# Expert rows and activations transposed by DMA on the SyncE queue, two blocks at a time, in a linear-attention and mixture-of-experts kernel

## The chip, the cores and the metric

The kernel runs on one core of a Trainium2 chip. The metric is the device time of one execution in microseconds (us). TensorE is called PE in the profile (PEld is its weight load), VectorE DVE, ScalarE ACT, GpSimd POOL, SyncE SP.

## The reference

Linear attention (8 batches, 8 heads, 576 positions, head size 64) feeds a mixture of 8 experts. Cut to what matters:

```python
k_p, q_p = phi(k), phi(q)             # relu(x)*cos and relu(x)*sin of the position
kv = einsum('bhsf,bhsd->bhfd', k_p, v); z = k_p.sum(axis=2)
attn = einsum('bhsf,bhfd->bhsd', q_p, kv) / (einsum('bhsf,bhf->bhs', q_p, z) + 1e-6)
x = attn.transpose(0, 2, 1, 3).reshape(4608, 512)
logits = x @ w_gate                   # 8 experts
e = argmax(logits); g = softmax(logits)[e]
# each expert takes at most 1152 tokens, in token order
out[i] = g[i] * (relu(x[i] @ w1[e]) @ w2[e])     # w1 512x1024, w2 1024x512; 0 if not taken
```

## The kernel before

All work is written as operations with a cost, a priority and the tiles that they read and write. A planner (`Plan.schedule`) simulates the engines with these costs, picks the order on each engine, and the program is emitted in that order. Each engine then runs its own list in order. `PHI` is a table of priority offsets by kind of operation. `Slots` is a pool of rotating buffers; a `Ver` is one use of a slot.

The attention works batch by batch. SP loads q, k and v of a batch (line 437, six loads of 576 KB). ACT and DVE scale k and v (lines 452 to 465), PE makes the key-value product (line 535), transposes q (line 493), and applies it (line 603); ACT and DVE bring the result to `num` (lines 613, 617). The routing (lines 658 to 764) finds each token's expert and its place; DVE writes the scaled rows as bf16 to `xg` (line 786), and POOL scatters them into a DRAM buffer `xd`, ordered by expert, 514 elements a row: 512 values and a row number (line 796).

The expert part works on 43 blocks of 128 rows. 20 blocks (table `a`) can be formed when six batches are scattered; the other 23 (table `b`) wait for the last two batches and for `pads`, eight writes of zero rows behind each expert's end (ACT, line 928). For each block:

- SP fetches 128 rows from `xd` into `xr` (line 994); POOL copies the row numbers out (line 998).
- PE transposes the rows, four 128x128 pieces (line 1003), and ACT or DVE copies them from PSUM to a unit buffer `un` (line 1007).
- For each half m of the 1024 hidden columns: PE multiplies with w1 (up, line 1023), ACT or DVE applies relu into `h` (lines 1032, 1034), PE transposes h (turn, line 1041), ACT or DVE copies it to `un` (line 1047).
- PE multiplies with w2 (down, line 1067), ACT or DVE copies the result (line 1072), POOL scatters it to the output (line 1081).

All ups come before the downs. The weights are cast to bf16 while POOL loads them, in halves of eight pieces of 512 KB each: w1a (line 945, during the attention), w1b (after the attention's buffers are given back, `swap`, line 1124), w2's first half (line 956), and w2's second half in w1a's place, once the last first-half up is done.

```python
def f_turn(m):
    def f():
        t_ps = tl(tvs[m], [P, 512], FP32, "ps")[:].bitcast(BF16)
        for x in range(4):
            nc.tensor.transpose(out=t_ps[:, x * P:(x + 1) * P], in_=hvs[m].tile[:, x // 2, x % 2, :],
                                identity=identb[:])
    return f
```

Of the kernel before, what the change touches and what calls it, by code (L numbers as in the profile page):

```python
# [28 lines left out]
    "G": 0.31, "KV": 0.33, "P": 0.35, "Q": -0.14, "T": -0.36, "carry": 1.34, "count": -1.01, "down": 0.6,  # L29
    "end": -3.84, "fetch": 0.26, "gout": 1.98, "ix": 1.87, "kva": 0.07, "load": -0.87, "pad": -0.91,  # L30
    "pre": -0.09, "relu": -1.78, "reluq": -0.77, "rq": 8.8, "scat": -0.24, "seen": -0.1, "tab": 0.69,
    "tmp": 1.28, "tsb": 1.62, "turn": -1.07, "up": -0.52, "vt": 17.49, "w1": 1.81, "w2": 0.68, "warm": -0.07,
    "wg": -0.36, "xT": -5.44, "xturn": -10.62,
# [3 lines left out]
class Slots:  # L37


    def __init__(self, name, n, fifo=True):  # L40
        self.name, self.n, self.fifo = name, n, fifo
        self.holder = [None] * n
        self.vers, self.given = [], 0

# [14 lines left out]
class Plan:  # L59
# [30 lines left out]
    def schedule(self, window=0.25, switch=0.15, sticky=0.6):  # L90
# [11 lines left out]
        while done < len(self.ops):  # L102
            best = {}
            cands = []
            for o in ready:
                t = o.avail
                ok = True
                for v in o.vers:
                    if v.slot is not None:
                        t = max(t, v.ready)  # L110
                    else:
                        ts = []
                        for h in v.slots.holder:
                            if h is None:
                                ts.append(0.0)
                            elif all(u.start is not None for u in h.uses):
                                ts.append(max(u.end for u in h.uses))
# [27 lines left out]
            for v in o.vers:  # L145
                if v.slot is None:
                    opts = []
                    for i, h in enumerate(v.slots.holder):
                        if h is None:
                            opts.append((0.0, i))  # L150
                        elif all(u.start is not None for u in h.uses):
                            opts.append((max(u.end for u in h.uses), i))
# [8 lines left out]
            if o.dma:  # L161
                dma_free = max(dma_free, o.end) + o.dma
                o.end = dma_free + 1.6
# [19 lines left out]
def kernel(  # L183
# [35 lines left out]
    U0, U1, U2 = 4, 41, 42  # L219
# [42 lines left out]
    xrS = Slots("xr", 4)  # L262
    hS, yS, uS = Slots("h", 4, False), Slots("y", 3, False), Slots("un", U0 + U1 + U2, False)
# [5 lines left out]
    v_t = [early.tile([P, HB * VH + HB * J * VX], FP32, name=f"v{i}") for i in range(vS.n)]  # L269
# [11 lines left out]
    nc.vector.memset(zrow[:], 0.0)  # L281

# [69 lines left out]
    for i in range(vS.n):  # L352
        nc.gpsimd.memset(v_raw(i)[:, :, VH - 2:VH], 0.0)
# [17 lines left out]
    identb = const.tile([P, P], BF16, name="identb")  # L371
# [17 lines left out]
    def count_1():  # L389
        nc.vector.tensor_scalar(out=m64_i[:], in0=col_i[:], scalar1=D - 1, scalar2=None, op0=ALU.bitwise_and)  # L390
        nc.vector.tensor_copy(out=m64[:], in_=m64_i[:])
        nc.vector.tensor_copy(out=identb[:], in_=ident[:])
# [27 lines left out]
    def load(b, name, u):  # L420
# [9 lines left out]
        def f():  # L430
            if name == "v":
                m = v_raw(ver.slot)[:, 2 * u:2 * u + 2, 0:J * D]
            elif name == "k":
                m = tl(ver, [P, HB, J, D], FP32, "early")[:, 2 * u:2 * u + 2, :, :].rearrange("p c j d -> p c (j d)")
            else:
                m = tl(ver, [P, 2, J, D], FP32, "early")[:].rearrange("p c j d -> p c (j d)")
# [5 lines left out]
    def attention(b):  # L442
# [37 lines left out]
        def q_relu(u, qr):  # L480
            def f():
                t = tl(qr, [P, J, 2, D], FP32, "early")
                nc.vector.tensor_scalar(out=t[:].rearrange("p j c d -> p c j d"), in0=loaded[b, "q", u].tile[:],  # L483
# [340 lines left out]
    def tab_ops(tag, n, b, prio):  # L824
# [17 lines left out]
        def add(fn, cost=0.1, **kw):  # L842
            keys = [("tab", tag)]
            op(kw.pop("eng", "DVE"), cost, fn, r=[("carry", b)] + kw.pop("r", []), w=keys + kw.pop("w", []), prio=prio,
               **kw).tag = ("tab", tag)
# [78 lines left out]
        def s_pad(e):  # L924
            def f():
                r0 = nc.values_load(T["end"][0:1, e:e + 1], engines=[ACTE], min_val=e * REG, max_val=e * REG + N,
                                    skip_runtime_bounds_check_because=INRANGE)
                zi = nc.scalar.dma_start(out=xd[bass.ds(r0, P), :], in_=zrow[:])
# [6 lines left out]
        for e in range(E):  # L935
            o = op("ACT", 0.95, s_pad(e), r=[("end",)], prio=prio, dma=0.4, after=[state["seen"]])
# [4 lines left out]
    def w1_load(n, e, prio, after):  # L941
        def f():
            if w1h[n] is None:
                w1h[n] = pools["mid"].tile([P, E, G, FH], BF16, name="w1b")
            nc.gpsimd.dma_start(out=w1h[n][:, e, :, :],
                                in_=moe_w1[e].rearrange("(g p) f -> p g f", p=P)[:, :, n * FH:(n + 1) * FH])
        op("POOL", 1.2, f, w=[("w1", n)], prio=prio, dma=2.95, after=after).tag = ("w1", n, e)
# [3 lines left out]
    def w2_load(n, e, prio, after):  # L951
# [6 lines left out]
        op("POOL", 1.2, f, w=[("w2", n)], prio=prio, dma=2.8, after=after).tag = ("w2", n, e)  # L958


    def unit(ver):

        if ver.tile is None:
            s = ver.slot
            where = "moe" if s < U0 else "mid" if s < U0 + U1 else "end"
            ver.tile = pools[where].tile([P, G, P], BF16, name=f"un{s}", tag=f"un{s}")
        return ver.tile

    def block(i):
        tag, n = ("a", i) if i < NA else ("b", i - NA)  # L970
        pr = 20.0 + i
        xv, yv, yp_ = Ver(uS), Ver(yS), Ver(pS)
        hvs, pvs, tvs, hts = ([Ver(s_), Ver(s_)] for s_ in (hS, pS, aS, uS))
# [18 lines left out]
        def f_fetch():  # L992
            xr = tl(xrv, [P, XW], BF16, "moe")
            early_read(nc.sync.dma_start(out=xr[:], in_=xd[bass.ds(row(SP), P), :]))

        def f_ids():
            ids["t"] = const.tile([P, 2], BF16, name=f"ids{i}")
            nc.gpsimd.tensor_copy(out=ids["t"][:], in_=xrv.tile[:, DT:XW])  # L998

        def f_xturn():  # L1000
            x_ps = tl(xpv, [P, 512], FP32, "ps")[:].bitcast(BF16)
            for g in range(G):
                nc.tensor.transpose(out=x_ps[:, g * P:(g + 1) * P], in_=xrv.tile[:, g * P:(g + 1) * P],  # L1003
                                    identity=identb[:])

        def f_xT(eng):
            (nc.scalar.copy if eng == "ACT" else nc.vector.tensor_copy)(  # L1007
                out=unit(xv)[:].rearrange("p g s -> p (g s)"), in_=xpv.tile[:].bitcast(BF16)[:, 0:DT])

        xrv, xpv = Ver(xrS), Ver(aS)  # L1010
        op("SP", 0.75, f_fetch, r=[("table", tag)], w=[("xr", i)], vers=[xrv], prio=pr - 10, dma=0.4,
           after=gate).tag = ("fetch", i)
        op("POOL", 0.15, f_ids, r=[("xr", i)], w=[("ids", i)], vers=[xrv], prio=pr).tag = ("ids", i)
        op("PE", 0.24, f_xturn, r=[("xr", i)], w=[("xps", i)], vers=[xrv, xpv], prio=pr - 3, mode="full",
           ).tag = ("xturn", i)
        op("ACT", 0.5, f_xT, r=[("xps", i)], w=[("xT", i)], vers=[xpv, xv], prio=pr - 3, alt=("DVE", 0.38)).tag = ("xT", i)

        def f_up(m):
            def f():
                e1 = expert()  # L1020
                hp = tl(pvs[m], [P, 2, 512], FP32, "ps")[:, 0, :]
                for g in range(G):
                    nc.tensor.matmul(out=hp, lhsT=xv.tile[:, g, :], rhs=w1h[m][:, bass.ds(e1, 1), g, :],  # L1023
# [3 lines left out]
        def f_relu(m):  # L1027
            def f(eng):
                h = tl(hvs[m], [P, 2, 2, P], BF16, "moe")
                src = pvs[m].tile[:, 0, :].rearrange("p (g q i) -> p g i q", g=2, i=2)  # L1030
                if eng == "ACT":
                    nc.scalar.activation(out=h[:], in_=src, func=ACT.Relu)  # L1032
                else:
                    nc.vector.tensor_scalar(out=h[:], in0=src, scalar1=0.0, scalar2=None, op0=ALU.max)
            return f

        def f_turn(m):
            def f():
                t_ps = tl(tvs[m], [P, 512], FP32, "ps")[:].bitcast(BF16)
                for x in range(4):  # L1040
                    nc.tensor.transpose(out=t_ps[:, x * P:(x + 1) * P], in_=hvs[m].tile[:, x // 2, x % 2, :],  # L1041
                                        identity=identb[:])
            return f

        def f_turned(m):
            def f(eng):
                (nc.scalar.copy if eng == "ACT" else nc.vector.tensor_copy)(  # L1047
                    out=unit(hts[m])[:].rearrange("p f s -> p (f s)"), in_=tvs[m].tile[:].bitcast(BF16)[:, 0:512])
            return f

        for m in range(2):
            pm = pr + 60 * m
            op("PE", 0.89, f_up(m), r=[("xT", i), ("w1", m)], w=[("h", i, m)], vers=[xv, pvs[m]], prio=pm, mode="full",
# [3 lines left out]
            op("PE", 0.24, f_turn(m), r=[("hr", i, m)], w=[("t", i, m)], vers=[hvs[m], tvs[m]], prio=pm - 3,  # L1057
               mode="full").tag = ("turn", i, m)
            op("DVE", 0.38, f_turned(m), r=[("t", i, m)], w=[("hT", i)], vers=[tvs[m], hts[m]], prio=pm,
               alt=("ACT", 0.5)).tag = ("hT", i, m)  # L1060
# [140 lines left out]
```

## Time and profile before

| | us |
|---|---|
| median of 3 runs | 362.04 (358.96 to 363.56) |
| profiled execution | 362.18 |
| its span | 360.4 |
| PE busy | 317.5 (88%) |
| ACT, DVE, POOL busy | 202.5, 187.3, 126.9 |
| mean granted PE clock | 0.965 |

The span runs from the first to the last instruction that the profiler saw; 1.8 us lie around it. A busy PE counts modelled ends of pipelined matmuls. Idle time of an engine that is not the bound costs nothing, so each stage is read by itself: the loads of the first batches, the attention, the ups, the downs.

### The profile page before, as it was taken

How to read it: one execution, taken by the hardware profiler on the slowest of the kernel's cores; microseconds unless marked ns; L12 is line 12 of the kernel's file. 1: busy time of each engine (PE TensorE's matmuls, PEld its weight loads, DVE VectorE, ACT ScalarE, POOL GpSimd, SP SyncE). 2: the span in 40 equal slices, each digit the busy share in tenths (PEclk: the TensorE clock that was granted, in tenths of full speed). 3: DMA queues.
4: the chain of work that ended last, by engine and by line, in shares of the span. 5: the costliest groups of instructions: out<-in, count | busy, mean ns of one | idle time of the engine just before them, and what ended most of it. 6: DMA issues, size and time to landing. Idle time of an engine off the chain costs nothing.

```text
span 360.4 us, 9576 instructions
## 1 busy us (share of the span) xinstructions
PE 317.5 (88%) x3344; PEld 208.9 (58%) x3368; DVE 187.3 (52%) x546; ACT 202.5 (56%) x450; POOL 126.9 (35%) x189
## 2 busy tenths in 40 slices
PE   5779798999989998883998889999999999999991
PEld 1668687878778787642555445555555444444440
DVE  5777889888898888787374435443333000000000
ACT  3588898989698754643444444555554333333330
POOL 5000424252807252657223222320000455555552
PEclk9899899999999899996899999999999999999997
DMA  4999939596995768599999996499100244342230
GB/s 156 394 391 387 344 118 341 181 360 144 382 292 191 119 120 132 148 179 246 207 225 213 215 201 124 76 211 211 27 3 0 94 162 156 146 163 113 92 132 0
DMA packets 38542, 66.62 MB, mean 185 GB/s; under 512 B 3903, under 2 KB 18655, under 8 KB 38498
## 3 DMA queue, kind: packets, MB, share of 16 engines
q0 software_dynamic: 18096, 31.00, 39.6%
q1 hardware_dynamic: 19250, 33.98, 27.4%
q10 hardware_dynamic: 1152, 1.05, 1.1%
q8 instruction: 29, 0.48, 0.5%
q14 instruction: 15, 0.12, 0.1%
HBM read 67.56 MB, written 17.06 MB: 235 GB/s over the span
## 4 chain that ended last, share of the span: by engine, by line
PE 43%; DMA 16%; ACT 10%; DVE 10%; issue 9%; POOL 7%; SPq 2%; ACTq 1%; POOLq 1%; DVEq 0%
PE p L1023 18%; PE p L1067 10%; PE p L603 7%; POOL out_dram L1081 6%; DMA xr<-xd 6%; PE a L1041 5%; DMA v<-in_v_dram 4%; DMA km<-in_k_dram 3%; ACT km L452 3%; DVE num L617 3%; DVE xg L786 2%; ACT v L463 2%; DMA w1a<-in_moe_w_dram 2%; PE a L1003 2%; DMA xd<-zrow 1%
## 5 line engine op out<-in xcount | busy, mean ns | idle before, releaser
L1067 PE MATMUL p<-w,un 128*128 x337 | 74.2, 379 | 0.5 <-issue 0.2
L796 POOL DMA_INDIRECT xd<-xg,si x40 | 45.4, 1135 | 81.9 <-DVE xg L786 64.8
L1032 ACT ACTIVATE h<-p 128x512 bf16<-128x512 f32 x65 | 38.9, 598 | 35.0 <-PE p L1023 32.2
L1067 PEld LDWEIGHTS <-un 128*128 128x128 bf16 x344 | 33.6, 98 | 40.4 <-issue 0.5
L603 PE MATMUL p<-kva,rq 64*128 64x146 f32 x640 | 51.7, 305 | 2.3 <-DVE num L617 0.6
L1072 ACT COPY y<-p 128x512 f32<-128x512 f32 x42 | 24.6, 585 | 48.0 <-PE p L1067 46.9
L1047 DVE COPY un<-a 128x512 bf16<-128x512 bf16 x66 | 27.9, 423 | 43.0 <-PE a L1041 42.9
L603 PEld LDWEIGHTS p<-kva,rq 64*128 64x128 f32 x640 | 44.8, 196 | 8.3 <-DVE num L617 4.6
L1023 PEld LDWEIGHTS <-un 128*128 128x128 bf16 x344 | 32.3, 98 | 28.9 <-issue 6.8
L1023 PE MATMUL p<-w1a,un 128*128 x162 | 43.8, 390 | 2.9 <-issue 1.4
L617 DVE SCALAR_TENSOR_TENSOR num<-p,tant,tmp 128x292 f32<-128x292 f32 (+1 forms) x80 | 39.9, 519 | 11.3 <-ACT tmp L613 10.7
L1023 PE MATMUL p<-w1b,un 128*128 x165 | 43.1, 378 | 1.1 <-issue 0.8
L535 PE MATMUL p<-v,km 64*64 64x132 f32 x1152 | 36.0, 279 | 5.7 <-DMA v<-in_v_dram 4.8
L1081 POOL DMA_INDIRECT out_dram<-y,ids x20 | 19.6, 979 | 58.9 <-ACT un L1047 44.6
L535 PEld LDWEIGHTS p<-v,km 64*64 64x64 f32 x1152 | 33.8, 136 | 7.9 <-issue 7.5
L613 ACT COPY tmp<-p 128x292 f32<-128x292 f32 (+1 forms) x77 | 30.8, 401 | 12.8 <-PE p L603 7.4
L1041 PEld LDWEIGHTS <-h 128*128 128x128 bf16 x344 | 25.2, 99 | 17.7 <-ACT h L1032 3.1
L1041 PE MATMUL a<-identb,h 128*128 128x128 bf16 x344 | 31.8, 221 | 0.7 <-ACT un L1007 0.5
L452 ACT ACTIVATE km<-km,cosn 128x256 f32<-128x256 f32 (+1 forms) x67 | 27.9, 485 | 1.9 <-DMA km<-in_k_dram 1.9
L1081 POOL DMA_INDIRECT out_dram<-y,ix x23 | 22.3, 972 | 16.9 <-ACT y L1072 16.9
L493 PE MATMUL a<-ident,qr 128*128 128x128 f32 x144 | 24.5, 291 | 3.1 <-DVE qr L483 1.2
L998 POOL COPY ids<-xr 128x2 bf16<-128x2 bf16 x43 | 8.8, 214 | 51.7 <-DMA xr<-xd 51.4
(169 smaller groups left out, 345.3 us busy)
## 6 DMA issues: line engine op xcount, KB each, us to landing
v<-in_v_dram SPq DMA_DIRECT2D x16, 576.0 KB, 8.8
km<-in_k_dram SPq DMA_DIRECT2D x16, 576.0 KB, 7.2
qm<-in_q_dram SPq DMA_DIRECT2D x16, 576.0 KB, 9.2
w<-in_moe_w_dram POOLq DMA_DIRECT2D x16, 512.0 KB, 8.1
xr<-xd SPq DMA_DIRECT2D x43, 128.5 KB, 5.2
w1a<-in_moe_w_dram POOLq DMA_DIRECT2D x8, 512.0 KB, 6.0
w1b<-in_moe_w_dram POOLq DMA_DIRECT2D x8, 512.0 KB, 8.8
xd<-zrow ACTq DMA_DIRECT2D x8, 128.5 KB, 7.3
```

The costliest lines, as they stand in the source:

```text
L452: nc.scalar.activation(out=kk, in_=kk, func=ACT.Relu, scale=cosn[:, j:j + 1])
L535: nc.tensor.matmul(out=kv_v[c * D:(c + 1) * D, 2 * o + u, :, :], lhsT=km.tile[rows, 2 * u + c, j, :], rhs=both, start=(j == 0), stop=(j == ...
L603: nc.tensor.matmul(out=p_ps[:, a, o, 0:2 * KW], lhsT=rq[u].tile[a * D:(a + 1) * D, o, col:col + P], rhs=kva.tile[a * D:(a + 1) * D, 2 * o ...
L613: (nc.scalar.copy if eng == "ACT" else nc.vector.tensor_copy)(out=t[0:rows], in_=by_t(0))
L617: nc.vector.scalar_tensor_tensor(out=num.tile[0:rows, c, u * HB:(u + 1) * HB, :], in0=by_t(1), scalar=tant[0:rows, c:c + 1], in1=tmp.tile[ ...
L796: si = nc.gpsimd.indirect_dma_start(out=xd[:, :], out_offset=bass.IndirectOffsetOnAxis(ap=xg.si[0:rows, c:c + 1], axis=0), in_=xg.tile[0:r ...
L1023: nc.tensor.matmul(out=hp, lhsT=xv.tile[:, g, :], rhs=w1h[m][:, bass.ds(e1, 1), g, :], start=(g == 0), stop=(g == G - 1))
L1032: nc.scalar.activation(out=h[:], in_=src, func=ACT.Relu)
L1041: nc.tensor.transpose(out=t_ps[:, x * P:(x + 1) * P], in_=hvs[m].tile[:, x // 2, x % 2, :], identity=identb[:])
L1047: (nc.scalar.copy if eng == "ACT" else nc.vector.tensor_copy)(out=unit(hts[m])[:].rearrange("p f s -> p (f s)"), in_=tvs[m].tile[:].bitcas ...
L1067: nc.tensor.matmul(out=y_ps, lhsT=hts[x // G].tile[:, x % G, :], rhs=w2h[x // G][:, bass.ds(e2, 1), x % G, :], start=(x == 0), stop=(x == ...
L1081: oi = nc.gpsimd.indirect_dma_start(out=out[:, :], out_offset=bass.IndirectOffsetOnAxis(ap=idx, axis=0), in_=yv.tile[:], in_offset=None, b ...
```

## The change

The row fetch becomes a transposing DMA from `xd` straight into a `un` buffer that holds two blocks. The row numbers are fetched by a DMA of their own on ACT's queue. The turn of h becomes a transposing DMA from SBUF to SBUF on SP, one for two blocks (256 KB), from `un` into one of six `h` buffers. The transposes on PE, their identity matrix and their PSUM copies go. The pads are issued by SP instead of ACT. The first k, v and q buffers (slot 0 of each) lie in a tile `big`, and w1's second half takes its place, so that its load no longer waits for the swap, only for the last use of these slots by the seventh batch; w1's first half is given earlier due times. The memset of v's pad columns goes from POOL to DVE, to the start. Slots with `fifo` take their buffers in fixed rotation. `PHI` has new values, and the planner adds an operation's latency after the DMA's end.

```diff
-    hS, yS, uS = Slots("h", 4, False), Slots("y", 3, False), Slots("un", U0 + U1 + U2, False)
+    hS, yS, uS = Slots("h", 6), Slots("y", 3, False), Slots("un", U0 + U1 + U2, False)
...
+    big = wp.tile([P, E * G * FH // 2], FP32, name="big")
+    assert VW + KWD + QW <= E * G * FH // 2
+    v_t = [big[:, 0:VW], early.tile([P, VW], FP32, name="v1")[:]]
...
+    for i in range(vS.n):
+        nc.vector.memset(v_raw(i)[:, :, J * D:VH], 0.0)
...
-    for i in range(vS.n):
-        nc.gpsimd.memset(v_raw(i)[:, :, VH - 2:VH], 0.0)
...
-                zi = nc.scalar.dma_start(out=xd[bass.ds(r0, P), :], in_=zrow[:])
+                zi = nc.sync.dma_start(out=xd[bass.ds(r0, P), :], in_=zrow[:])
...
-                w1h[n] = pools["mid"].tile([P, E, G, FH], BF16, name="w1b")
+                assert all(loaded[b, x].slot for x in "kv") and all(loaded[b, "q", u].slot for u in range(2))
+                w1h[n] = big[:].bitcast(BF16).rearrange("p (e g f) -> p e g f", e=E, g=G)
...
         def f_fetch():
-            xr = tl(xrv, [P, XW], BF16, "moe")
-            early_read(nc.sync.dma_start(out=xr[:], in_=xd[bass.ds(row(SP), P), :]))
+            early_read(nc.sync.dma_start_transpose(out=unit(xv)[:, k, :, :], in_=xd[bass.ds(row(SP), P), 0:DT]))
 
         def f_ids():
             ids["t"] = const.tile([P, 2], BF16, name=f"ids{i}")
-            nc.gpsimd.tensor_copy(out=ids["t"][:], in_=xrv.tile[:, DT:XW])
...
+            early_read(nc.scalar.dma_start(out=ids["t"][:], in_=xd[bass.ds(row(ACTE), P), DT:XW]))
...
-        op("SP", 0.75, f_fetch, r=[("table", tag)], w=[("xr", i)], vers=[xrv], prio=pr - 10, dma=0.4,
+        op("SP", 1.3, f_fetch, r=[("table", tag)], w=[("xT", i)], vers=[xv], prio=pr - 10, lat=1.0, dma=0.5,
            after=gate).tag = ("fetch", i)
...
         def f_turn(m):
             def f():
-                t_ps = tl(tvs[m], [P, 512], FP32, "ps")[:].bitcast(BF16)
-                for x in range(4):
-                    nc.tensor.transpose(out=t_ps[:, x * P:(x + 1) * P], in_=hvs[m].tile[:, x // 2, x % 2, :],
-                                        identity=identb[:])
...
+                nc.sync.dma_start_transpose(
+                    out=tl(hts[m], [P, 2, G, P], BF16, "moe")[:, 0:k + 1].rearrange("p k f s -> p (k f) s"),
+                    in_=hvs[m].tile[:, 0:k + 1].rearrange("p k g q -> p (k g q)"))
             return f
...
     for e in range(E):
-        w1_load(0, e, e + 0.1, ops_of("KV", min(4 + e // 2, B - 1)))
+        w1_load(0, e, e + 0.1, ops_of("load", "q", 1 + 3 * e // 4, 1))
     for e in range(E):
-        w1_load(1, e, 50.0 + e, [swapped])
+        w1_load(1, e, 50.0 + e, ops_of("KV", B - 2) + ops_of("reluq", B - 2))
...
     for e in range(E):
-        w2_load(0, e, 60.0 + e, [swapped, *[o for o in ops_of("up", 4 * e + 4) if o.tag[2] == 0]])
+        w2_load(0, e, 60.0 + e, [*ops_of("w1", 1), *[o for o in ops_of("up", 4 * e + 8) if o.tag[2] == 0]])
```

In the changed program the order of SP is: all q/k/v loads, 13 fetches, the eight pads, 30 fetches, then the 44 turns.

## The prediction

> **What bounds the kernel now.** I read the page's first two parts (busy shares and slices), then the busy time by stretch, then the chain of work that ended last, then the groups of instructions, and last the waits of SyncE's own queue.
>
> ```profile
> span 360.4 us, 9576 instructions
> PE 317.5 (88%) x3344; PEld 208.9 (58%) x3368; DVE 187.3 (52%) x546; ACT 202.5 (56%) x450; POOL 126.9 (35%) x189
> GB/s 156 394 391 387 344 118 341 181 360 144 382 292 191 119 120 132 148 179 246 207 225 213 215 201 124 76 211 211 27 3 0 94 162 156 146 163 113 92 132 0
> ```
>
> TensorE is busy 88% of the span. The GB/s row (9 us a slice) shows one stretch that is not TensorE's: slices 2 to 5 move 344 to 394 GB/s, the highest of the run.
>
> ```profile
> 150.00:170.00 20.00, 11.90 (x102) 7.42 (x105) 16.95 (x56) 9.23 (x19) 14.21 (x23) 0.86 0.93 201
> 170.00:232.00 62.00, 56.26 (x429) 32.41 (x436) 29.32 (x81) 28.99 (x52) 14.73 (x43) 0.96 0.95 183
> 232.00:278.00 46.00, 45.00 (x323) 25.78 (x329) 18.04 (x43) 24.31 (x42) 4.77 (x7) 1.00 0.51 92
> 278.00:352.70 74.70, 74.22 (x341) 33.74 (x347) 0.95 (x2) 24.87 (x44) 40.89 (x42) 1.00 0.34 127
> ```
>
> Columns: stretch, length, busy PE, PEld, DVE, ACT, POOL, then clock, DMA share, GB/s. From 232 us to 352.7 us TensorE is the bound outright (45.0 of 46.0, 74.2 of 74.7). From 170 to 232 it is nearly so; from 150 to 170 it is not.
>
> ```profile
> L1041 PE MATMUL a<-identb,h 128*128 128x128 bf16 x344 | 31.8, 221 | 0.7 <-ACT un L1007 0.5
> L1067 PE MATMUL p<-w,un 128*128 x337 | 74.2, 379 | 0.5 <-issue 0.2
> L1003 PE MATMUL a<-identb,xr x172: 216/219/314, 144.6 to 227.0; 128*128 128x128 bf16 x172
> L994 SPq DMA_DIRECT2D xr<-xd x43: 332/333/377, 139.2 to 222.6; - x43
> DMA to landing us min/median/max: 2.0/5.2/6.7
> ```
>
> So 344 + 172 = 516 transposes run on TensorE in the expert part, all between 144 and 279 us. A plain row fetch costs SyncE 0.33 us and lands after 2.0 to 6.7 us.
>
> ```profile
> 8.09 12.73 DMA v<-in_v_dram
> 20.84 12.42 DMA km<-in_k_dram
> SPq L437 <- POOL v L353: 3.2, 1, 3.2
> ```
>
> Up to 33.3 us the chain is k and v loads; after that it is computation up to 140 us, but for one w1a load at 98 us, beside which PE stays 87% busy (8.65 of 10.0 us), so little hangs on it. The first load waits 3.2 us for GpSimd's memset of the v pads and is issued at 3.90 us.
>
> [...]
>
> **The change, part by part.** *Transposes leave TensorE.* In 232 to 278 us I count 156 weight loads of L1023 (39 up groups of four) and 171 of L1041 (43 turns). A down group of eight takes 74.7 / 43 = 1.74 us, so four matmuls take 0.87. 39 x 0.87 = 33.9, and 46.0 - 33.9 = 12.1 us for 43 turns: 0.28 each, with their gaps. Call it 0.26 to 0.28. The expert part has 86 turns and 43 row transposes: 129 x 0.27 = 35 us off the bound engine.
>
> *The up stage now.* It runs from 153 to 278 us, 125 us. The ups alone are 86 x 0.87 = 75 us, the transposes 35, the counting matmuls 1; 14 us are stalls, of which 7.05 is one wait at 161 to 168 us for the pad writes that ACT issues and the fetches behind them. After: 75 to 77 us of ups, 1 of counting, and I keep 6 of stalls, because half of w1 arrives earlier, in the place of the first buffers, and first-block second halves can fill that hole. That is 84 us: 41 us less.
>
> *Copies off ACT and DVE.* 129 PSUM evacuations go (L1007 and L1047 at 0.42 to 0.60 us), about 62 us in all. They lie beside TensorE, so I count nothing. ACT takes on 43 loads of row numbers; each is a table read, a move and an issue as on L994 today, about 0.72 us, 31 us of ACT's queue. With 62 relus at 0.60 that is 68 us in an 84 us stage: hidden by TensorE, but a relu stuck behind a load[...] stalls the three PSUM buffers. It is in the 6 us.
>
> *Pads to SyncE.* Eight pads at about 0.88 us move from ACT, where they cost the 7 us hole, to SyncE between the 13th and 14th fetch. The fetches behind wait; TensorE has second halves of 13 blocks (12 us) in the meantime. Nothing on the path.
>
> *Start.* The v-pad memsets move to DVE right after zrow (ends 1.14 us), so the first load goes at about 1.4 instead of 3.9 us: -2.5. But in the changed instruction order on GpSimd three w1a loads stand right behind its setup, with no wait ahead of them: issued from 6 us, in the saturated stretch. Eight w2 loads alone, 230 to 260 us, used 0.83 + 1.12 + 0.39 slices of 10 us, so 2.9 us each: +8.8. Sum +6.3 on a chain that is loads, then computation with no slack. [...] I take +6.
>
> *Second half of w2.* It takes w1a's place, so it starts after the last first-half up. In the changed order 21 ups remain, 21 x 0.87 = 18 us, while eight loads at 2.9 take 23: the first down waits about 4 us more. Today 46 us of ups cover it.
>
> *The turns as DMAs.* 43 fetches, and 44 turns of two blocks (256 KB), all on SyncE. Six buffers hold three pairs; in the down stage each pair needs two turns, and its buffers come free when the downs of three pairs before are done. TensorE needs 2 x 1.74 = 3.5 us a pair[...]. [...] I take 1.3 us a turn: hidden. If 2.6, a pair takes 5.2 us.
>
> *Sum* against the profiled execution, 360.4 us of span and 362.2 in all: 360.4 + 6 - 41 + 4 = 329 us, down stage and 7.7 us tail as today; with 1.8 around it 331. The median of the runs, 362.0, is the same as that execution's time, so no correction.
>
> **The rivals.** *B, slower: SyncE's sequencer becomes the bound of the down stage.* [...] Three pairs are turned ahead; the other 19 follow[...]. Same formula, level with today at (105.7 - 7.2) / 18.5 = 5.3 us a pair: it decides from 2.6 us a turn. For it:[...] all turns stand in one queue behind one another. [...]
>
> *C, turns at 1.8 to 2.5 us:* a pair takes 3.6 to 5.0 us, the stage 78 to 100 us: 334 to 356, say 346 us.
>
> *D, the ups are starved:* fetches at 3 us each on SyncE make 43 x 3 = 129 us from 144 us on, ups end at 275 rather than 241: 331 + 34 = 365 us, no change. Against: SyncE idles for 32 us before the first fetch today, and PE has second halves to fill.
>
> **How the numbers follow.** Chances: forecast (318 to 340) 0.46, C 0.16, D 0.06, B 0.32. Forecast 331. The range goes to 316 below (no penalty for the early w1a, no stalls) and to 392 above, so that B at its price is in; about 0.18 is left out[...]. The forecast's own range is 318 to 342. A difference under 2%, 7 us, is about what a measurement of this kernel can't tell from none. Faster by over 2% is the forecast, and most of C: 0.56. Within 2%: D and the dear end of C: 0.08. Slower: 0.36, B and the bad end of D.
>
> **What would show it.** Right: no transposes on PE; up groups 0.9 us apart; downs 1.74 us apart with PE over 95% busy to the end; first load issued near 1.4 us; km of the third batch landing near 39 us; turns that take SyncE under 1.7 us. Wrong: PE idle before L1075 with the DMA of h as releaser, and turns back to back on SyncE at over 2.6 us (B), or idle before L1038 with the fetch as releaser (D).

## The result, and the profile after

The changed kernel takes 402.27 us (median of 4 runs, 398.89 to 409.19) where the kernel before took 362.80 us beside it (358.96 to 364.68): ratio 1.110, 95% interval 1.095 to 1.124. It is slower by 40 us; the forecast was 331. The profiled execution took 409.19 us, the longest of the four, with a span of 407.4 us; it and four profiled ones below (without stores; ids loads on GpSimd; the same with w1a late; fetches alone with ids on GpSimd) are slow ones, 1.8 to 2.8% above the fastest of their kernel, so their stage times are some us too long, and the ratios leave slow executions out.

The page of the changed kernel, first the lines that answer to those shown of before:

```profile
span 407.4 us, 8518 instructions
PE 311.9 (77%) x2837; PEld 187.6 (46%) x2852; DVE 157.7 (39%) x472; ACT 171.9 (42%) x396; POOL 117.9 (29%) x144
DMA  7999978997892999379994455706959999999980
DMA packets 107370, 77.84 MB, mean 191 GB/s; under 512 B 78239, under 2 KB 87487, under 8 KB 107330
q1 hardware_dynamic: 83042, 46.29, 49.3%
```

TensorE has about 500 matmuls less to do and is busy for hardly less time (311.9 us instead of 317.5); its share fell from 88% to 77% of a longer span. What grew is the DMA: a row of nines in the last quarter, where the kernel before had its DMA engines two thirds idle, and 78,239 packets under 512 bytes. Of the kernel before the same two lines read:

```profile
DMA packets 38542, 66.62 MB, mean 185 GB/s; under 512 B 3903, under 2 KB 18655, under 8 KB 38498
q1 hardware_dynamic: 19250, 33.98, 27.4%
```

Busy time by the same stretches as in the prediction (columns as there: PE, PEld, DVE, ACT, POOL, clock, DMA share, GB/s):

```profile
150.00:170.00 20.00, 12.71 (x114) 9.19 (x115) 10.14 (x31) 6.26 (x17) 0.98 (x1) 0.83 0.88 123
170.00:232.00 62.00, 31.09 (x123) 11.85 (x124) 20.45 (x65) 10.73 (x20) 15.19 (x18) 0.78 0.82 154
232.00:278.00 46.00, 36.31 (x139) 14.51 (x142) 11.45 (x31) 12.08 (x21) 0.00 (x0) 0.89 0.41 71
278.00:352.70 74.70, 64.31 (x260) 26.46 (x263) 0.00 (x0) 25.30 (x43) 27.38 (x30) 0.93 1.03 193
```

From 170 to 232 us TensorE is busy half the time (31.1 of 62), where it had 56.3; and in the last row, where it had been busy 74.2 of 74.7, the DMA share is now 1.03. So there are two losses in two places. Where each stage ends (the start of the last score product, which ends TensorE's part of the attention, of the last up product and of the last down product):

| | last score product | last up | last down |
|---|---|---|---|
| before | 150.4 | 277.2 | 352.2 |
| changed | 165.6 (+15.2) | 296.6 | 398.6 |
| length of the stage, before / changed | | 126.8 / 131.0 | 75.0 / 102.0 |

The groups of the changed kernel name TensorE's waits (behind the second bar), and the answers on its two DMA lines give how long one DMA holds SyncE (ns, min/median/max):

```profile
L1075 PE MATMUL p<-w,h 128*128 x337 | 83.5, 398 | 18.5 <-DMA h<-un 8.6
L1038 PE MATMUL p<-w1a,un 128*128 x167 | 46.1, 411 | 39.3 <-ACT un L1047 35.9
L1054 SPq DMA_TRANSPOSE h<-un x44: 1243/1932/3827, 252.0 to 391.6; - x44
L1023 SPq DMA_TRANSPOSE un<-xd x43: 1188/1196/5959, 146.0 to 250.8; - x43
```

The downs (L1075) wait for the turned h. The first-half ups (L1038, w1a) wait 35.9 us for ScalarE's relu (L1047). A turn holds SyncE 1.93 us at the median, a fetch 1.20, but up to 5.96.

Each load of row numbers is called an ids load from here on. The timeline of ScalarE and SyncE in the worst of it, with TensorE's lines:

```profile
186.94 30.70 SPq L1023 DMA_TRANSPOSE un<-xd  x10
194.18 21.54 ACTq L1027 DMA_DIRECT2D ids<-xd  x3
215.76 0.60 ACT L1047 ACTIVATE un<-p 128x512 bf16<-128x512 f32 x1 [25.53 <-issue]
216.41 1.87 PE L1038 MATMUL p<-w1a,un 128*128 x4 [22.06 <-ACT un L1047]
225.02 9.91 ACTq L1027 DMA_DIRECT2D ids<-xd  x4
235.37 0.60 ACT L1047 ACTIVATE un<-p 128x512 bf16<-128x512 f32 x1 [10.26 <-DMA un<-xd]
236.02 5.13 PE L1038 MATMUL p<-w1a,un 128*128 x15 [6.42 <-ACT un L1047]
```

Three ids loads of 0.5 KB, each of which takes ScalarE 0.35 us to issue (median of the 43), take up 21.5 us of its queue while ten fetches take 30.7 us of SyncE's beside loads of w2. The relu behind them starts late, and TensorE, whose buffers in PSUM the relus empty, stands 22 us: this is "the hole" below. The rest of the 35.9 us comes later, from 216 to 252 us, where the mean DMA share is only 0.45 and SyncE issues a fetch every 1.6 us: ScalarE's ids loads still wait for fetches to land (10.26 us before one relu), and TensorE waits another 13.5 us in three pieces. So full DMA engines make this harm worse, but it is there without them too, with fetches that hold SyncE their shortest 1.19 us. Followed back from its end, the changed kernel's chain of work runs through SyncE's fetches, one behind another, from 187 to 250 us.

### The profile page after: what moved, and what is told of

Read it like the earlier page. It is cut to its first block, busy times and chain, and to the rows that moved or that the text cites. A ratio compares the mean times of both kernels' runs of the same rounds, so it can differ in the third digit from the quotient of the medians.

```text
span 407.4 us, 8518 instructions
## 1 busy us (share of the span) xinstructions
PE 311.9 (77%) x2837; PEld 187.6 (46%) x2852; DVE 157.7 (39%) x472; ACT 171.9 (42%) x396; POOL 117.9 (29%) x144
## 2 busy tenths in 40 slices
DMA packets 107370, 77.84 MB, mean 191 GB/s; under 512 B 78239, under 2 KB 87487, under 8 KB 107330
## 4 chain that ended last, share of the span: by engine, by line
issue 20%; SPq 16%; POOL 10%; PE 5%; DMA 3%; POOLq 1%; DVE 1%; ACTq 0%; ACT 0%
SPq L1023 12%; POOL out_dram L1089 10%; PE p L1038 5%; SPq L1010 2%; DMA w<-in_moe_w_dram 1%; SPq L948 1%; DMA xd<-xg,si 1%; DMA un<-xd 1%; POOLq L1089 1%; SPq L946 1%; DVE xg L806 0%; POOL w L979 0%; ACTq L1027 0%; POOLq L1204 0%; ACT un L1047 0%
## 5 line engine op out<-in xcount | busy, mean ns | idle before, releaser
L1075 PE MATMUL p<-w,h 128*128 x337 | 83.5, 398 | 18.5 <-DMA h<-un 8.6
L1038 PEld LDWEIGHTS <-un 128*128 128x128 bf16 x344 | 34.9, 102 | 94.6 <-issue 60.2
L1038 PE MATMUL p<-w1a,un 128*128 x167 | 46.1, 411 | 39.3 <-ACT un L1047 35.9
L1047 ACT ACTIVATE un<-p 128x512 bf16<-128x512 f32 x62 | 36.7, 597 | 91.7 <-PE p L1038 32.5
L1075 PEld LDWEIGHTS <-h 128*128 128x128 bf16 x344 | 34.8, 101 | 67.5 <-issue 23.1
L637 DVE SCALAR_TENSOR_TENSOR num<-p,tant,tmp 128x292 f32<-128x292 f32 (+1 forms) x80 | 39.1, 516 | 22.5 <-ACT tmp L633 22.2
L1038 PE MATMUL p<-big,un 128*128 x169 | 44.3, 397 | 1.7 <-issue 1.0
L1049 DVE TENSOR_SCALAR un<-p 128x512 bf16<-128x512 f32 x24 | 16.6, 692 | 71.7 <-PE p L1038 71.5
L806 DVE TENSOR_TENSOR xg<-num,rden 128x512 bf16<-128x512 f32 (+1 forms) x40 | 24.7, 685 | 0.6
L520 ACT COPY rq<-a 128x512 f32<-128x512 f32 (+1 forms) x47 | 21.7, 479 | 4.9 <-DMA un<-xd 2.5
L555 PE MATMUL p<-big 64*64 64x132 f32 x576 | 18.8, 289 | 3.0 <-DMA big<-in_v_dram 3.0
L513 PEld LDWEIGHTS a<-ident,qr 128*128 128x128 f32 x144 | 17.8, 156 | 5.3 <-ACT rq L520 1.7
L555 PEld LDWEIGHTS p<-big 64*64 64x64 f32 x576 | 17.9, 142 | 4.3 <-issue 4.2
## 6 DMA issues: line engine op xcount, KB each, us to landing
w1a<-in_moe_w_dram POOLq DMA_DIRECT2D x8, 512.0 KB, 10.4
```

What stands on the lines that cost most here:

```text
L513: nc.tensor.transpose(out=q_ps[:, n * P:(n + 1) * P], in_=qr.tile[:, j, :, :].rearrange("p c d -> p (c d)"), identity=ident[:])
L555: nc.tensor.matmul(out=kv_v[c * D:(c + 1) * D, 2 * o + u, :, :], lhsT=km.tile[rows, 2 * u + c, j, :], rhs=both, start=(j == 0), stop=(j == ...
L637: nc.vector.scalar_tensor_tensor(out=num.tile[0:rows, c, u * HB:(u + 1) * HB, :], in0=by_t(1), scalar=tant[0:rows, c:c + 1], in1=tmp.tile[ ...
L1038: nc.tensor.matmul(out=hp, lhsT=xv.tile[:, k, g, :], rhs=w1h[m][:, bass.ds(e1, 1), g, :], start=(g == 0), stop=(g == G - 1))
L1047: nc.scalar.activation(out=h, in_=src, func=ACT.Relu)
L1075: nc.tensor.matmul(out=y_ps, lhsT=hts[x // G].tile[:, k, x % G, :], rhs=w2h[x // G][:, bass.ds(e2, 1), x % G, :], start=(x == 0), stop=(x ...
```

## The experiments

Kernels ran in six groups on chips whose times for the kernel before lie between 362.6 and 372.3 us, so ratios to that kernel are what is compared between groups. "Ends" below are the last score product, last up and last down, as in the table.

### The turns in the down stage: the DMA engines' time or SyncE's sequencer?

**Without the output stores of the first 40 blocks**, the changed kernel otherwise:

```
+                if i < 40:
+                    return
                 idx = ids["ix"][:] if i >= NA else ids["t"][:].bitcast(I32)
```

> The changed kernel without the output stores of all blocks below the 40th (left out: those rows of the output are not written). Theory 2 (the down stage is bound by the time of the 16 DMA engines: two turns at about 1.9 us of all engines each and two output stores at 0.6 us each a pair): the stage falls from about 103 us to 80 to 85 us, the program to about 380 us, and the turns' landing shortens. Rival (SyncE's sequencer is held by issuing each turn, whatever else moves): the stage stays at 100 to 104 us and the program at about 402. The up stage is unchanged under both.

Measured: 379.87 us, ratio 1.044 (1.038 to 1.050). Ends 167.3, 298.1, 378.2: the down stage is 80 us instead of 102, and the up stage as it was.

**Turns as plain copies:**

```
-                nc.sync.dma_start_transpose(
-                    out=tl(hts[m], ...)[:, 0:k + 1].rearrange("p k f s -> p (k f) s"),
+                nc.sync.dma_start(
+                    out=tl(hts[m], ...)[:, 0:k + 1].rearrange("p k f s -> p (k f s)"),
```

> The changed kernel with the 44 turns as plain copies by DMA of the same tiles at the same places (left out: the transposition of h, so the down products are of other numbers). Theory 2 (the transposed turns cost 1.5 to 1.9 us of all 16 DMA engines for 256 KB and fill them together with the output stores): the stage falls from 102 us to about 80, DMA share in it to 0.75 or less, the program to about 380 us. Rival (any 256 KB moved by DMA in that stage, plain or transposed, fills the engines with the stores): the stage stays above 95 us.

Measured: 391.14 us, ratio 1.056 (1.048 to 1.063) in a group where the kernel before took 370.3. Ends 169.2, 298.5, 379.5: again 81 us for the down stage, with all stores in it. (1.056 of the first group's 362.8 us would be 383 us.) The products are of other numbers here, since h is not transposed.

DMA queues in the 60 us from 305 to 365 us, turns on q1 and stores on q0. The changed kernel (26 turns issued), the one without stores (34), the one with plain turns (34):

```profile
q1 hardware_dynamic: 25485, 6.33, 77.5%
q0 software_dynamic: 1992, 6.49, 35.7%
h<-un SPq DMA_TRANSPOSE x26, 5.8
```

```profile
q1 hardware_dynamic: 34538, 8.58, 86.1%
h<-un SPq DMA_TRANSPOSE x34, 3.1
```

```profile
q1 hardware_dynamic: 4672, 8.52, 39.3%
q0 software_dynamic: 2557, 7.97, 35.6%
h<-un SPq DMA_DIRECT2D x34, 256.0 KB
```

A transposed turn takes 0.861 x 60 / 34 = 1.52 us of all 16 engines when it is alone and 0.775 x 60 / 26 = 1.79 beside the stores; a plain copy of the same 256 KB takes 0.393 x 60 / 34 = 0.69, with the stores beside it. In the changed kernel turns and stores add to 113% of the engines (packets overlap). SyncE's part, without stores:

```profile
L1054 SPq DMA_TRANSPOSE h<-un x44: 1188/1266/2342, 253.6 to 370.7; - x44
```

The sequencer needs 1.27 us a turn at the median. Two of them fit into TensorE's 3.5 us a pair; with the stores in place it is 1.93. So SyncE's sequencer alone is not the bound. Either edit, taking away the stores or the transposing, brings the stage down to 80 us, where TensorE is the bound again (busy 59.7 and 60.0 of these 60 us, instead of 50.4, with the DMA share at 0.87 and 0.75, instead of 1.14): the stage was bound by the DMA engines' time.

**Turns on TensorE**, at the same places in the order:

```
-                nc.sync.dma_start_transpose(out=tl(hts[m], ...), in_=hvs[m].tile[...])
...
+                for x in range(4 * (k + 1)):
+                    nc.tensor.transpose(out=t_ps[:, x * P:(x + 1) * P],
+                                        in_=hvs[m].tile[:, x // 4, x % 4, :], identity=identb[:])
+                nc.vector.tensor_copy(out=tl(hts[m], ...), in_=t_ps[:, 0:n])
```

> The changed kernel with the turns (h from units in rows to units in partitions) done by TensorE, eight transposes into one PSUM bank and one VectorE copy, at the same places in the order, where the change does them by one DMA transpose on SyncE. Theory 2/4 (the DMA turns bound the down stage): the stage falls from 103 us to about 95 us, 44 turns of 8 transposes at 0.11 us on TensorE added, DMA share in the stage back to some 36%, the program to about 394 us. Rival (something that is not the turn slows the down stage, the output stores or VectorE): the stage is 103 us or more, since 44 copies and 344 transposes are added to engines.

Measured: 396.35 us, ratio 1.093 (1.086 to 1.099). Ends 161.3, 292.0, 384.9: the down stage is 93 us, TensorE busy 59.6 of the 60 us from 305 on. So putting the work back on the engine that was full costs less than the DMA did. Against the 75 us of the kernel before, whose down stage has no turns, 86 turns of one block's half cost 18 us, 0.21 each, with eight transposes in a row.

### The up stage: who holds ScalarE?

**Ids loads on GpSimd's queue:**

```
-            early_read(nc.scalar.dma_start(out=ids["t"][:], in_=xd[bass.ds(row(ACTE), P), DT:XW]))
+            early_read(nc.gpsimd.dma_start(out=ids["t"][:], in_=xd[bass.ds(row(mybir.EngineType.Pool), P), DT:XW]))
```

> The changed kernel with one edit: the 43 small ids loads of the blocks are issued on GpSimd's queue instead of ScalarE's. Theory 1 (in the up stage ScalarE's in-order queue stands behind an ids load[...]; its relus and so the PSUM buffers stand with it): the 22 us hole of TensorE at 194 to 216 us goes, the ups end some 25 to 30 us before 296.7, the program takes about 375 us. Rival (the fetched transposes themselves come too late, one pair in 1.6 us of queue and longer in the crowded stretch): TensorE waits for the un tiles instead, and the gain is under 5 us (398 to 402). The down stage is unchanged at about 103 us under both.

Measured: 383.44 us, ratio 1.051 (1.045 to 1.058), 19 us less than the changed kernel. Ends 154.2, 279.9, 375.9. The 30 us from 190 to 220, changed kernel and then this one:

```profile
190.00:220.00 30.00, 7.80 (x27) 3.04 (x27) 2.77 (x4) 0.83 (x2) 0.28 (x1) 0.64 1.01 179
```

```profile
190.00:220.00 30.00, 21.31 (x75) 8.13 (x77) 11.58 (x35) 2.98 (x5) 13.44 (x23) 0.83 1.10 148
```

The hole is gone. Of the attention's delay 11.4 us are gone between these two profiles, and 7.1 against the kernel with turns on TensorE, whose attention is the changed one and ends at 161.3. But the gain is less than expected, and the up stage is still 125.7 us long: TensorE now waits 8.0 us there for fetched rows, and 17.1 us before second-half ups for relus of ScalarE, which in its turn waits there for turns that have not landed (21.3 us in three waits, the longest 10.4).

**Fetches as plain row loads**, ids loads still on ScalarE:

```
-            early_read(nc.sync.dma_start_transpose(out=unit(xv)[:, k, :, :], in_=xd[bass.ds(row(SP), P), 0:DT]))
+            early_read(nc.sync.dma_start(out=unit(xv)[:, k, :, :].rearrange("p g q -> p (g q)"), in_=xd[...]))
```

> The changed kernel with the fetches as plain row loads into the same tiles (left out: the transposition of x, so the products are of other numbers; ids loads stay on ScalarE, turns stay DMA transposes). Theory 1 (the ids loads on ScalarE are late[...]): the hole at 194 to 216 us goes with the transposes, attention ends some 8 us earlier, the program at 370 us or less. Rival (ScalarE's stall comes from w2's first half, 8 loads of 2.9 us in the same stretch, whatever the fetches are): the hole stays at 15 us or more and the program is over 390 us.

Measured: 378.91 us, ratio 1.039 (1.028 to 1.051). Ends 157.1, 269.2, 367.8. The hole shrinks to one wait of 7.4 us. The same ids loads on the same queue do much less harm beside plain fetches, which hold SyncE 0.33 us each: it takes both. (Here, too, the products are of other numbers.)

### The early loads of w1a

```
+    for e in range(E):
+        o = ops_of("w1", 0, e)[0]
+        plan.order.remove(o)
+        plan.order.insert(plan.order.index(ops_of("KV", min(4 + e // 2, B - 1))[-1]) + 1, o)
```

> The changed kernel with the three loads of the first half of w1 put back after the K/V of batches 4, 4 and 5, as in the kernel before, where the change issues them at the start. Theory 3 (they take 2.9 us each of a saturated load stretch from the attention): TensorE's last attention work and SyncE's end of the gathers at 145 us come 7 to 9 us earlier, the program 5 to 9 us shorter (about 395). Rival (the attention is later for other reasons, the change's fetches beside it): both within 1 us of the changed kernel.

The edit moves all eight loads, of which the changed kernel issues three at 6 us. Measured: 403.67 us, ratio 1.105 (1.093 to 1.116): no change. Ends 162.8, 293.0, 392.8: the score products end 2.8 us before those of the changed kernel's profile, but 1.5 after those of the kernel with turns on TensorE, which has the early loads. The hole stands in its ups as before (22.2 us). **With the ids loads on GpSimd as well:**

> The changed kernel with two edits: ids loads on GpSimd's queue and w1a's loads late; turns still by DMA. Against the kernel with all three edits this prices the DMA turns alone. If the turns stand in the DMA engines' queue behind w2's loads and the stores: 15 to 22 us more than the kernel with all three edits, that is about 378 us. If the turns cost only their down stage: about 4 us more than that kernel.

Measured: 384.71 us, ratio 1.045 (1.034 to 1.056), with ends 146.7, 279.8, 375.3. Here the attention ends 7.5 us before that of the ids kernel and 3.7 us before that of the kernel before (in the next kernel, whose attention is the same, it ends at 150.7, so one profile gives this to some 4 us). The ups end at the same time as in the ids kernel: whatever the attention gains, the up stage does not use.

### The three causes together

Ids loads on GpSimd, w1a late, turns on TensorE:

> The changed kernel with three edits together: ids loads on GpSimd's queue (-19 us alone), w1a's loads after the K/V of batches 4 to 5 (0 alone, since the hole behind the ids loads took up what the attention gained), turns on TensorE (-6 us alone). Only the fetched DMA transposes, the place of w1's second half and the pads remain of the change. If the three causes are separate: attention done at about 149 us (before 150.4, the ids kernel 154.2), no stall of ScalarE behind a turn while w2's second half is loaded (16 us in the ids kernel), down stage at about 92 us: about 360 us, level with the kernel before. Rival (the fetched transposes alone hold the up stage at 125 us even then): about 372 us.

Measured: 372.50 us, ratio 1.023 (1.016 to 1.031): the rival's number. Ends 150.7, 266.1, 360.9. Against the kernel with DMA turns (1.045) this prices those turns at 2.2%, 8 us, between the two expectations. In the profiles it lies in the ups, 115 us long instead of 133: with DMA turns TensorE waits there twice 8.1 us for a relu of ScalarE, and ScalarE for turns (24.7 us in four waits) while turns hold SyncE for up to 11.2 us beside the loads of w2's second half. The down stage is 95 us in both. What is left of the up stage's waits:

```profile
L1041 PE MATMUL p<-w1a,un 128*128 x172 | 44.5, 404 | 13.6 <-DMA un<-xd 11.7 <-DVE ix L1094 1.2 <-issue 0.5
L1041 PE MATMUL p<-big,un 128*128 x172 | 44.1, 396 | 12.9 <-DMA ids<-xd 11.7 <-DVE un L1052 0.7 <-issue 0.4
```

11.7 us wait for fetched x; 11.7 us are one wait before the first product with w1's second half, which the trace puts down to an ids load. **The same kernel with each ids load behind its block's second relu:**

```
+    for i in range(NBLK):
+        o = ops_of("ids", i)[0]
+        plan.order.remove(o)
+        plan.order.insert(plan.order.index(ops_of("relu", i, 1)[-1]) + 1, o)
+        for o in ops_of("ix", i): ...   # to just before the block's down
```

> The changed kernel with w1a late, turns on TensorE and ids loads on GpSimd, these last now behind the second relu of their block (the same kernel with them among the fetches: ratio 1.023, TensorE 11.7 us before its first product with w1's second half, 11.7 us waiting for un tiles). If the first of these waits came from the ids loads in GpSimd's queue: 8 to 12 us less, ratio 0.99 to 1.00. If it is the landing of w1's second half beside the fetches: no change, ratio 1.02.

Measured: ratio 1.013 (1.002 to 1.023), beside 1.023 (1.016 to 1.031): the intervals overlap, so this run tells the two apart poorly. In its profile the wait before the first product with w1's second half is 6.8 us instead of 11.7, and an ids load holds TensorE elsewhere (6.2 us in the ups, 2.7 in the downs).

### The fetches alone, on the kernel before

**The v pads zeroed early** is the base for what follows:

```
+    for i in range(vS.n):
+        nc.vector.memset(v_raw(i)[:, :, J * D:VH], 0.0)
...
-    for i in range(vS.n):
-        nc.gpsimd.memset(v_raw(i)[:, :, VH - 2:VH], 0.0)
```

> The kernel before with one small part of the change: the zeroing of the two v pads is done by VectorE at the start, not by GpSimd after its other work. The prediction's step 5 has -2.5 us for it (3.2 us of SyncE's wait for GpSimd go): about 360 us; the rival, that the load stretch is bound by the DMA engines from there on and takes it back, 363 us (no change). Either within what a measurement can tell only with care; the start of the first scores in the trace decides.

Measured: 361.51 us, ratio 0.994 (0.991 to 0.997). The first load goes at 1.19 us instead of 3.89; by the ratio about 2 of these 2.7 us arrive at the end (1 to 3). **With the pads issued by SyncE too:**

```
-                zi = nc.scalar.dma_start(out=xd[bass.ds(r0, P), :], in_=zrow[:])
+                zi = nc.sync.dma_start(out=xd[bass.ds(r0, P), :], in_=zrow[:])
```

> The kernel before with two small parts of the change: the v pads zeroed early on VectorE, and the eight pad rows' stores of xd issued by SyncE instead of ScalarE, planned anew. In the kernel with the early zeroing alone a ScalarE copy stands 7.9 us behind the pads' DMAs and TensorE waits 5.6 us for it at 168 us. If that wait goes and SyncE's fetches behind the pads are not missed: 3 to 5 us less, about 357 us (ratio to before 0.985). The prediction's step 4 says nothing changes (ratio 0.994, as with the early zeroing alone), since the fetches then wait for the pads on SyncE as the copies did on ScalarE.

Measured: ratio 0.994 (0.991 to 0.997), the same. These two beat both kernels, by half a percent; neither fetches nor turns by DMA transpose.

**The fetches as DMA transposes**, on the base with the early zeroing, ids loads on GpSimd and then on ScalarE, planned anew (`eng` is `gpsimd`, then `scalar`):

```
-            early_read(nc.sync.dma_start(out=xr[:], in_=xd[bass.ds(row(SP), P), :]))
+            early_read(nc.sync.dma_start_transpose(out=unit(xv)[:], in_=xd[bass.ds(row(SP), P), 0:DT]))
-            nc.gpsimd.tensor_copy(out=ids["t"][:], in_=xrv.tile[:, DT:XW])
+            early_read(nc.<eng>.dma_start(out=ids["t"][:], in_=xd[bass.ds(row(...), P), DT:XW]))
...
-        op("PE", 0.24, f_xturn, ...)
-        op("ACT", 0.5, f_xT, ..., alt=("DVE", 0.38))
```

> One part of the change alone, on the kernel before with the v pads zeroed early (361.5 us): x is fetched by DMA transposes on SyncE, its 43 groups of TensorE transposes (16.4 us busy in that kernel) and their copies go, the ids come by small loads on GpSimd; turns on TensorE, w1 and w2 as before, order planned anew. If the fetches are hidden behind TensorE's work: about 350 us. Rival (landing of 4 to 20 us and a queue that takes 1.2 to 5 us a fetch give TensorE as much waiting as the transposes cost): 358 to 368 us, with waits of the ups for un tiles.

> As the kernel with the fetches alone, ids loads on ScalarE's queue as in the change. Theory 1 (ids loads on ScalarE hold the relus): 15 us or more above the GpSimd variant. Rival (only the changed kernel's own order puts the ids loads in a bad place): within 4 us of it.

Measured: 406.43 us, ratio 1.094 (1.085 to 1.103), and 424.12 us, ratio 1.144 (1.134 to 1.155). ScalarE costs 17.7 us more than GpSimd, as theory 1 said. But both are far above the expected 350 to 368, and the new plan is part of that: in the first, GpSimd's loads of w1's second half stand behind a w2 load that waits 28.2 us for TensorE, and TensorE then waits 22.8 us for w1. **Ids loads moved behind the second relu:**

```
+        op("POOL", 0.6, f_ids, r=[("table", tag), ("hr", i, 1)], w=[("ids", i)], prio=pr + 60, ...)
```

> The kernel with the fetches alone (DMA transposes of x; turns on TensorE; planned anew), its ids loads on GpSimd moved behind the second relu of their block, so that neither w1's and w2's loads nor ScalarE stand behind an ids load while the fetches run. It was at ratio 1.094 to the kernel before with the ids loads among the fetches. If only the ids loads did the harm, and the fetches are hidden: the 16 us of TensorE's transposes of x are saved, ratio 0.96 to 0.98. If the fetched transposes themselves cost what they save (their landing, their share of the DMA engines beside the loads of w1 and w2): ratio 0.99 to 1.03, with waits of the ups for un tiles.

Measured: ratio 1.050 (1.038 to 1.062), better than 1.094 and outside both expectations. Its timeline shows the same trap with other DMAs in it, the pad stores that ScalarE issues in this kernel (line 928, as in the kernel before):

```profile
162.65 17.42 ACTq L928 DMA_DIRECT2D xd<-zrow  x8
180.16 1.09 ACT L1015 ACTIVATE h<-p 128x512 bf16<-128x512 f32 x2 [22.19 <-DMA xd<-zrow]
180.82 0.61 PE L1024 MATMUL a<-identb,h 128*128 128x128 bf16 x4 [18.10 <-ACT h L1015]
```

So the last pair: **that kernel with the pads on SyncE**, and **the same order with the fetches as plain row loads**.

> The kernel with the fetches alone and its ids loads late, with the eight pad stores also moved from ScalarE to SyncE: no engine that computes now issues a DMA among the fetched transposes. In the one with pads on ScalarE that engine stood 22.2 us behind them (ratio 1.050). If the harm came from ScalarE's and GpSimd's queues alone: ratio 0.97 to 0.99, for TensorE no longer transposes x. If the fetched transposes themselves use up what is saved: 1.00 to 1.02, with ups that wait for un tiles and for w1's second half.

> The same kernel with the fetches as plain row loads into the same tiles (left out: the transposition of x, so the products are of other numbers). The difference is what the transposing in the DMA costs there: if it is only the queue's 1.2 us a fetch, hidden, under 3 us less; if the transposed packets' time on the DMA engines holds back the loads of w1 and w2 and the rows: 8 to 15 us less (ratio 0.95 to 0.97).

Measured: 382.42 us, ratio 1.052 (1.045 to 1.060), and 354.49 us, ratio 0.977 (0.971 to 0.984). With the pads on SyncE TensorE waits 5.7 us for ScalarE's relus instead of 21.7, and yet the ratio is what it was: it waits 27.6 us for fetched rows instead of 7.3. Between the two kernels of the pair one form of instruction differs, and 28 us. Ends 147.8, 300.7, 375.8 against 146.4, 272.5, 347.6: nearly all of it is in the ups. TensorE's group, then SyncE's fetches in the crowded stretch, transposed and plain (duration on SyncE min/median/max, first and last start, then the landing):

```profile
L1006 PE MATMUL p<-w1a,un 128*128 x165 | 52.5, 450 | 32.0 <-DMA un<-xd 27.6 <-DVE xg L786 1.6 <-issue 1.5
L993 SPq DMA_TRANSPOSE un<-xd x12: 1189/3344/4599, 168.9 to 209.5; - x12
DMA to landing us min/median/max: 4.8/15.9/17.0
```

```profile
L1006 PE MATMUL p<-w1a,un 128*128 x165 | 46.7, 410 | 13.1 <-DMA un<-xd 7.6 <-DVE xg L786 2.2 <-issue 2.0
L993 SPq DMA_DIRECT2D un<-xd x33: 332/333/549, 165.1 to 204.8; - x33
DMA to landing us min/median/max: 5.9/10.6/12.3
```

Beside loads of w1's second half and w2's first, SyncE starts 12 transposed fetches in 40.6 us, one in 3.4 us, and 33 plain ones in 39.7 us, one in 1.2 us; the DMA engines are full in both (share 1.23 and 1.18 from 170 to 190 and from 190 to 210 us, and 1.14 and 1.16 with plain fetches). TensorE needs 0.87 us for the up of a block and waits ten times for 27.6 us in all, 20 us more than with plain fetches. The granted clock is lower in this stretch as well (0.50 from 170 to 210 us; with plain fetches 0.74 up to 190 and 1.00 after), and the products that do come run slower: 1.87 us for four instead of 1.02. TensorE's first-half ups and its turns are busy 7.7 us longer (52.5 + 36.0 us against 46.7 + 34.1). Together that is about the 28 us.

## Why the prediction was wrong, step by step

Its sum had 329 us for the span; the profile has 407.4. The stages close the account: attention 9.2 over the +6, ups 45 over (131.0 instead of 126.8 - 41 = 85.8), downs 27 over of which the +4 for w2 is already in the sum: 329 + 9.2 + 45 + 23 = 406. Two steps failed: the stalls of the up stage, put at 6 us, and the turns, called hidden.

- **Transposes leave TensorE, 35 us.** The size was somewhat high for the turns, where it was measured: 0.21 us each (eight transposes in a row, the kernel with turns on TensorE) for 0.27. Their worth was too high as well. In the nearest comparison, the kernel with late ids and plain fetches stands 1.7% under the one with x transposed on TensorE (0.977 to 0.994), about 6 us for the 43 row transposes, net of the ids loads and of another order, where my count gives 43 x 0.27 = 11.6. Against that stand 28 us for transposing in the DMA.
- **The up stage now, 84 us with 6 us of stalls: the step that failed most.** I took the stalls from today's holes and called a relu behind a load "in the 6 us" without pricing it. TensorE waited 35.9 us for such relus, and taking the ids loads off ScalarE gave 19 us of the program. And I named 3 us for a fetch only in rival D and never asked what it is beside loads of 512 KB, where the DMA is already at 0.95: 3.4 us. In the changed kernel itself TensorE waits only 0.9 us for a fetched row, since ScalarE's wait comes first; with the ids loads moved it is 7 to 28 us. That the ups then starve was rival D, with 3 us a fetch: 0.06 was too little for it, and the reason against it ("SyncE idles for 32 us before the first fetch") spoke only of a time before the crowd.
- **Copies off ACT and DVE, 0; ACT's ids loads hidden.** No run tests the first by itself. The second was a sum of busy time (68 of 84 us) for a queue that is in order: it says nothing of what one blocked instruction holds up. The trace names the landing of fetches as what ScalarE waited for (10.26 us in the line above), and both a queue change and plain fetches take the wait away. Why an ids load waits for a fetch that it does not read, no run isolates.
- **Pads to SyncE, nothing.** Held: 0.994 with and without. With transposed fetches the move takes away the 22.2 us stall above, but not the time (1.050 and 1.052).
- **Start, -2.5 and +8.8.** The first load goes 2.7 us earlier, and about 2 arrive, as said. The price of the early w1a loads is not settled: with the ids loads on GpSimd the attention ends at 154.2 with them and at 146.7 and 150.7 without, 3.5 to 7.5 us; with the ids loads on ScalarE it ends at 161.3 with them and at 162.8 without. What the sum lacked here is ScalarE: its ids loads hold the attention as well (7 to 11 us). And "a chain with no slack" failed: the program gains nothing from w1a late, since the ups behind it have another bound. (The prediction's reading that slices 2 to 5 move the most is not exact: slices 9 and 11, with 360 and 382 GB/s, move more than slice 5.)
- **Second half of w2, +4.** Held: the changed kernel waits 3.5 us for it in the downs.
- **The turns, 1.3 us each, hidden: the other step that failed.** The price on the queue, which is the planner's cost of a turn in the changed kernel, was right (1.27 us without the stores). What was wrong is the time of the DMA engines: the profile of before has no DMA transpose that could price it, and I asked only what one turn takes, not what two turns and two stores take of the same 16 engines. A turn took 1.52 us of them, 172 GB/s, and 1.79 us, 146 GB/s, beside the stores. Two turns at 1.79 us and two stores at 0.357 x 60 / 26 = 0.82 us are 5.2 us of packet time, partly overlapped; a pair took 102 / 22 = 4.6 us. The 0.34 that the stores take stood in the very row that I showed for TensorE's 74.2 of 74.7 us: 25 us. With the 38 turns that start in this stage that makes 52 us at the 0.69 of a plain copy, still inside the 75, and 83 us at 1.52: the sum alone would not have shown it, it needs the measured price too. Rival B was in the right place with the wrong resource (it decides from 2.6 us of SyncE a turn, and 1.27 was measured; its own price was shown by no run); rival C was near for the pair (3.6 to 5.0 us, measured 4.6), but gave no reason for its price, and B's formula, 3.5 + 18.5 x (us a pair) + 3.7, makes 74 us of 3.6 us a pair, not 78.
- **The chances.** I treated B, C and D as alternatives to the forecast and to each other. Two of them happened at once, in two stages, and add up; the range's upper end was one of them alone. (Its two ranges for the forecast, 318 to 340 and 318 to 342, differ by a slip.)

What no run takes apart: w1's second half in the place of the first buffers was not tried by itself, nor the new `PHI` and the fixed rotation of buffers, and whether transposed fetches lose to the weight loads for their small packets (27,983 under 512 bytes in the last pair's first kernel, 5,279 with plain fetches) or for something else, stays open.

## What to carry to other kernels

Before work is moved from a full engine to the DMA, sum the DMA engines' time in the stage where it lands, with everything that already moves there; a share of 0.34 or 0.95 in the profile of before is the start of that sum (the 0.34 became 1.03 here), and an issue time is not. Measure the new transfer's own engine time first, beside such traffic. Do not issue small DMAs from an engine whose next instruction empties PSUM while slow transfers are queued: each engine runs its list in order, and here three blocked loads of 0.5 KB stopped TensorE for 22 us. And rivals in different stages are not alternatives: add them.

## What the hardware showed that I had not expected

Transposing in the DMA cost at least 2.2 times the engine time of a plain copy of the same tile (1.52 us alone against 0.69 beside stores, for 256 KB). A transposed fetch of 128 KB held SyncE 1.19 us where the DMA engines had room and 3.3 us at the median, up to 4.6, beside weight loads, and its landing went from 2.8 us (222 to 246 us in the changed kernel) to 15.9. And the granted clock was low where TensorE waited: 0.50 with TensorE busy 6.7 of 20 us, and still 0.50 in the next 20 us with 11.7, where the kernel with plain fetches, busy 15.6 and 16.5, had 0.74 and 1.00.
